# Two groups mixed side by side: q of odd groups on the other half of the partitions, heads collected by halves and crossed once a batch

## The chip, the cores and the metric

The kernel runs on one core of one Trainium2 chip. The metric is device time in microseconds, taken as the median of several runs; lower is better. PE is TensorE, DVE is VectorE, ACT is ScalarE, POOL is GpSimd and SP is SyncE, which here only issues DMAs.

## The reference

Inputs are `u` and `v` (8 batches, 3200 rows, 256 columns), `z` (8, 3200, 64), and the weights `w_q`, `w_k` (256 x 64) and `w_out` (256 x 256), all fp32. For each batch:

```python
attn  = np.maximum(z @ z.T / S, 0) ** 2        # 3200 x 3200
x     = u * (attn @ v)                         # 3200 x 256
q, k  = x @ w_q, x @ w_k                       # 3200 x 64 each
mixed = (q @ k.T / 8) @ x                      # 3200 x 256
out   = np.maximum(mixed, 0) @ w_out
```

There is nothing between q, k and x in the third step that is not linear, so `mixed` is computed as q times the small matrix k.T @ x (64 x 256), which the kernel calls the heads.

## The kernel before

**Stages.** A batch has 3200 rows, cut into 25 blocks of 128 rows and into seven groups: six of 512 rows (0 to 5) and one of 128 (6, `LASTG`). In text, batches are numbered 0 to 7. The main loop runs over phases `k`, some 22 to a batch, in an order that is written out by hand in Python. In a phase, in program order:

- a *mix* of an older batch, if one is due (line 416): its PSUM goes through relu on ACT (`mix_out`, line 428) to a tile `rt`;
- six score matmuls (four in a phase with a mix), in pairs into one PSUM tile (line 211);
- their relu and scale on DVE or ACT into `g` (lines 230, 234), one phase later their square on POOL or ACT into `at` (lines 247, 249);
- the second product, attention times v, from `at` tiles of about two phases earlier or from DMA-transposed ones (`tt`), accumulated in `acc` (line 289). After its first ten matmuls comes an extra: in a phase with a mix the projection of the mixed group with `w_out` (`proj`, line 441; written out by ACT, line 468); in others, where due, `keys_and_heads`;
- when a group of rows is complete, two `gate` operations on DVE multiply by u into `x_sb` (line 315), which frees the `acc` tiles; a DMA transposes `x_sb` into `xT_sb` (line 327).

**Keys, queries and heads.** `keys_and_heads` takes one group, or groups 5 and 6 together. The projection matmuls (line 337) give q on partitions 0 to 63 and k on 64 to 127 of one PSUM tile; ACT copies it to `qk` (line 348), and a DMA transposes that to `kx`, with q in the first 64 columns and k in the last (line 353). At the next key step, `double_keys_queries` has SP copy by DMA the lower half of `qk` over its upper half, so that q stands on both halves (line 361), and POOL copies k over the q columns of `kx` (line 362). The heads matmuls (line 368) then give k.T @ x on both halves. The running sum `ha` is kept by DVE (lines 379, 381); the last addition of a batch gives `hs` in fp16 (line 387), with the same 64 rows on both halves. These DVE operations read the same PSUM tile as ACT's copy to `qk`, and in the trace they start after it.

**Mixes.** A mix takes one group. Two matmuls with 64 contraction rows run on the two halves of the array side by side: columns 0 to 127 of the heads on the lower half, 128 to 255 on the upper. A batch has six, three phases apart or more; the first comes in the phase after the one that makes `hs`. Group 6 is mixed on the side, in the spare columns of a later key step's PSUM tile (`side_mix`, line 481), with all 128 partitions, so that its sum is twice too large and the relu scales by 0.5.

**Slots.** A pool gives each new tile the slot of an older one, and the first writer waits until the older tile's last reader is done. `ps` has three PSUM slots for scores, keys, mixes and projections. `pq` has nine for `qk`, one for each group of seven a batch; `pk` three for `kx`, `prt` three for `rt`.

**The last batch and the tail.** In the last batch a key step comes three phases after its group instead of five, and mixes wait until more than two are listed. After the loop, three mixes of batch 6 are left; they and their projections fill PE while the last groups of batch 7 are gated, transposed and added to its heads by way of x.T @ x (`last_gram`, `last_heads`). Then batch 7 is mixed and projected group by group, with DVE writing out.

Of the kernel before, what the change touches and what calls it, by code (L numbers as in the profile page):

```python
# [9 lines left out]
FP16 = mybir.dt.float16  # L10
FP32 = mybir.dt.float32
RELU = mybir.ActivationFunctionType.Relu
AOP = mybir.AluOpType
# [3 lines left out]
def kernel(  # L17
# [45 lines left out]
    ptt = ctx.enter_context(tc.tile_pool(name="ptt", bufs=1))  # L63
    psml = ctx.enter_context(tc.tile_pool(name="psml", bufs=2))
    pq = ctx.enter_context(tc.tile_pool(name="pq", bufs=9))
    prt = ctx.enter_context(tc.tile_pool(name="prt", bufs=3))
    pps = ctx.enter_context(tc.tile_pool(name="pps", bufs=3, space=bass.MemoryType.PSUM))
    pacc = ctx.enter_context(tc.tile_pool(name="pacc", bufs=1, space=bass.MemoryType.PSUM))

    def ps_tile(name):  # L70
        return pps.tile([P, 2, W], FP32, tag="ps", name=name)
# [77 lines left out]
    wq32 = consts.tile([P, ND, dh], FP32, tag="wq32", name="wq32")  # L149
    wk32 = consts.tile([P, ND, dh], FP32, tag="wk32", name="wk32")  # L150
    wqk = consts.tile([P, ND, 2, dh], FP16, tag="wqk", name="wqk")
    wq2 = consts.tile([P, ND, 2, dh], FP16, tag="wq2", name="wq2")
    wk2 = consts.tile([P, ND, 2, dh], FP32, tag="wk2", name="wk2")
    wo = consts.tile([P, ND, D], FP16, tag="wo", name="wo")
# [8 lines left out]
    def cast_weights():  # L163
        nc.gpsimd.tensor_copy(out=wqk[:, :, 0, :], in_=wq32[:])
        nc.gpsimd.tensor_copy(out=wqk[:, :, 1, :], in_=wk32[:])
        for half in range(2):
            nc.gpsimd.tensor_copy(out=wq2[:, :, half, :], in_=wq32[:])
            nc.gpsimd.tensor_copy(out=wk2[:, :, half, :], in_=wk32[:])
        nc.gpsimd.tensor_copy(out=wo[:], in_=wo32[0][:])
# [174 lines left out]

    def projections_out(b, gi, out):
        gw = widths[gi]
        qks[b, gi] = pq.tile([P, W], FP16, tag="qk", name="qk")
        nc.scalar.copy(out=qks[b, gi][:, 0:gw], in_=out)  # L348

    def turn_keys(b, gi):  # L350
        gw = widths[gi]
        ks[b, gi] = pk.tile([P, 4, 2, dh], FP16, tag="kx", name="kx")
        nc.sync.dma_start_transpose(
            out=ks[b, gi][:, 0 : gw // P, :, :].rearrange("p n a h -> p n (a h)"),
            in_=qks[b, gi][:, 0:gw],
        )

    def double_keys_queries(b, gi):
        gw = widths[gi]
        nn = gw // P  # L360
        nc.sync.dma_start(out=qks[b, gi][dh:P, 0:gw], in_=qks[b, gi][0:dh, 0:gw])
        nc.gpsimd.tensor_copy(out=ks[b, gi][:, 0:nn, 0, :], in_=ks[b, gi][:, 0:nn, 1, :])  # L362

    def heads(b, gis, ps, stop=True):

        parts = [(gi, n) for gi in gis for n in range(widths[gi] // P)]
        for gi, n in parts:
            nc.tensor.matmul(  # L368
                out=ps[:, 1, 0:D],
                lhsT=ks[b, gi][:, n, :, :].rearrange("p a h -> p (a h)"),  # L370
                rhs=xs[b, gi][:, n, :],
                start=((gi, n) == parts[0]),
                stop=(stop and (gi, n) == parts[-1]),
            )

    def heads_out(b, gis, ps):
        if gis[0] == 0:
            hacc[b] = psml.tile([P, D], FP32, tag="ha", name="ha")
            nc.vector.tensor_copy(out=hacc[b][:], in_=ps[:, 1, 0:D])
        elif gis[-1] < LASTG:  # L380
            nc.vector.tensor_add(out=hacc[b][:], in0=hacc[b][:], in1=ps[:, 1, 0:D])  # L381
        else:
            heads_done(b, ps[:, 1, 0:D])

    def heads_done(b, part):
        hss[b] = psml.tile([P, D], FP16, tag="hs", name="hs")
        nc.vector.tensor_add(out=hss[b][:], in0=hacc.pop(b)[:], in1=part)  # L387

    def last_gram(b, gi, ps):
        nj = widths[gi] // P  # L390
# [10 lines left out]
    def last_heads(b, g32, ps):  # L401
        for cc in range(ND):
            nc.tensor.matmul(
                out=ps[:, 1, 0:D],
                lhsT=wk2[:, cc, :, :].rearrange("p t h -> p (t h)"),
                rhs=g32[:, ds(cc * D, D)],
                start=False,
                stop=(cc == ND - 1),
            )

    def mix(b, gi):
        gw = widths[gi]
        ps = ps_tile("mx")
        for db in range(ND):
            half = db * dh
            nc.tensor.matmul(  # L416
                out=ps[:, db, 0:gw],
                lhsT=hss[b][half : half + dh, ds(db * P, P)],
                rhs=qks[b, gi][half : half + dh, 0:gw],
                start=True,  # L420
                stop=True,
            )
        return ps

    def mix_out(b, gi, ps):
        gw = widths[gi]
        rts[b, gi] = prt.tile([P, ND, W], FP16, tag="rt", name="rt")
        nc.scalar.activation(out=rts[b, gi][:, :, 0:gw], in_=ps[:, :, 0:gw], func=RELU)  # L428

    def proj(b, gi, banks=None):  # L430
        rt = rts.pop((b, gi))
# [47 lines left out]
    def side_mix(b, ps):  # L479
        for db in range(ND):  # L480
            nc.tensor.matmul(
                out=ps[:, 1, ds(D + db * P, P)],
                lhsT=hss[b][:, ds(db * P, P)],
                rhs=qks[b, LASTG][:, 0:P],
                start=False,
                stop=(db == ND - 1),
            )

    def side_mix_out(b, ps):
        rts[b, LASTG] = prt.tile([P, ND, P], FP16, tag="rs", name="rs", bufs=2)  # L490
        nc.scalar.activation(
            out=rts[b, LASTG][:].rearrange("p a s -> p (a s)"), in_=ps[:, 1, D : 2 * D],
            func=RELU, scale=0.5,
        )
        side.append((side_proj, side_proj_out, b))

# [13 lines left out]
        nc.sync.dma_start(out=rows(out, b)[:, NT - 1, :], in_=fo[:])  # L510


    todo_mix, todo_between, at_phase, side = [], [], {}, []
    keyed, keyed_at = [], [-9]

    def due(k, fn):
# [11 lines left out]
    def keys_and_heads(b, gis):  # L528

        ps = ps_tile("qk")  # L530
        outs = [ps[:, 0, 0:W], ps[:, 1, D : D + P]]
        projections(b, gis[0], wqk, outs[0])
        aside = None
        if keyed:
            heads(*keyed[0], ps, stop=(len(gis) == 1 and not side))
            if len(gis) > 1:
                projections(b, gis[1], wqk, outs[1], start=False)
            elif side:
                aside = side.pop(0)
                aside[0](aside[2], ps)  # L540
        for gi, o in zip(gis, outs):
            projections_out(b, gi, o)
            turn_keys(b, gi)
        if keyed:
            hb, hgis = keyed.pop(0)
            heads_out(hb, hgis, ps)
            if hgis[-1] == LASTG:
                todo_mix.extend((hb, i) for i in range(LASTG))
                side.append((side_mix, side_mix_out, hb))
        if aside:  # L550
            aside[1](aside[2], ps)
        keyed.append((b, gis))
        keyed_at[0] = now[0]
# [47 lines left out]
    while groups:  # L601
# [3 lines left out]
        n = 4 if k == 0 else 6  # L605
        mixing = None
        if mix_due(k):
            mb, mg = todo_mix.pop(0)
            mixed_at[0] = k
            mixing = (mb, mg, mix(mb, mg))  # L610
            n = 4
        n = min(n, NTILE - produced)
        fresh = []
# [2 lines left out]
        produced += n  # L616
        made_by.append(produced)
        keying = not mixing and key_due(k)
        if keying and keyed:
            for g_ in keyed[0][1]:  # L620
                double_keys_queries(keyed[0][0], g_)
        if mixing:
            mix_out(*mixing)
        staged = []
        act_pair = 0 if (gate_pending or k < 4) else 1
        for i, (p0, sc) in enumerate(fresh):
# [51 lines left out]
        gate_pending = False  # L678
        matmuls = second_product(b, gi, rows_, begins, closes)
        extra = None  # L680
        if mixing:
            mb, mg, _ = mixing

            def extra():
                proj_out(mb, mg, proj(mb, mg), [(False, nc.sync, widths[mg] // P)])
        elif keying:
            extra = todo_between.pop(0)[1]
# [26 lines left out]

    assert not at_phase and not side and not todo_between and len(keyed) == 1
    hb, hgis = keyed.pop()
    for g_ in hgis:
        double_keys_queries(hb, g_)
    psh = ps_tile("hd")
    heads(hb, hgis, psh, stop=False)  # L720
    last_gram(last, LASTG, psg)
    g32 = pg.tile([P, ND * D], FP32, tag="g", name="G")
    nc.scalar.copy(out=g32[:, 0:D], in_=psg[:, 0:D])
    nc.vector.tensor_copy(out=g32[:, D : 2 * D], in_=psg[:, D : 2 * D])
    for mb, mg in todo_mix[:2]:
        mix_out(mb, mg, mix(mb, mg))
    last_heads(last, g32, psh)
    heads_done(last, psh[:, 1, 0:D])
    for mb, mg in todo_mix[2:]:
        mix_out(mb, mg, mix(mb, mg))  # L730

    def store(b, gi, banks=None, ways=None):
        proj_out(b, gi, proj(b, gi, banks), ways or [(True, nc.sync, widths[gi] // P)])

    for i, (mb, mg) in enumerate(todo_mix):
        if i == 0:
            store(mb, mg, [acc_tile(0, "fo0")[:], acc_tile(1, "fo1")[:]],
                  [(True, nc.sync, 2), (True, nc.sync, 2)])
        else:
            store(mb, mg)  # L740
    qs = [(LASTG - 1, ps_tile("qq")[:, 0, :]), (LASTG, acc_tile(0, "qq")[:, 0:P])]
    for gi, o in qs:
        projections(last, gi, wq2, o)
    for gi, o in qs:
        projections_out(last, gi, o)
    mix_out(last, 0, mix(last, 0))
    for gi in range(LASTG - 1):
        mix_out(last, gi + 1, mix(last, gi + 1))
        if gi == LASTG - 2:
            mix_out(last, LASTG, mix(last, LASTG))  # L750
        store(last, gi)
    store(last, LASTG)
    store(last, LASTG - 1, ways=[(False, nc.scalar, 2), (True, nc.sync, 2)])

# [29 lines left out]
```

## Time and profile before

| | |
|---|---|
| median of 3 runs | 807.75 us (806.59 to 809.63) |
| profiled execution | 807.18 us, of which the span is 805.4 us |
| TensorE clock granted, mean | 0.999 of full speed |
| instructions in the span | 16696 |
| DVE, ACT, POOL busy | 493.1, 475.1, 485.2 us |
| DMA q over the upper half (line 361) | 54 issues |
| POOL copy of k (line 362) | 54, 20.4 us busy together |

In a line of the profile's timeline the first number is the start in the span and the second the time to the end of the last instruction of the line, then engine, source line, operation, output<-inputs, shape and count. In brackets stand the idle time of that engine before it and what ended that. Matmuls are pipelined: one of 256 columns shows 0.27 us, but a row of them moves on by about 0.11 us each. PEld is the weight load of TensorE. A line of waits has engine, line and releaser, then us in total, times, and the longest.

### The profile page before, as it was taken

What the parts mean: (1) busy time and instruction counts of PE and PEld (TensorE: products, weight loads), DVE (VectorE), ACT (ScalarE), POOL (GpSimd) and SP (SyncE); (2) the same over time, 40 slices, a digit from 0 to 9 for tenths busy, and PEclk for the clock granted to TensorE, in tenths of its full rate; (3) what the DMA queues carried; (4) which work ended last, traced back from release to release, by engine and by line L of the source; (5) the groups of instructions that cost most, each with busy time, mean ns of one, the idle gap of its engine ahead of it and who ended that gap; (6) DMA issues with size and microseconds to landing.
All of it is one profiled execution on the core that took longest, in us unless ns stands there. A gap on an engine that the chain in (4) does not pass through costs nothing.

```text
span 805.4 us, 16696 instructions
## 1 busy us (share of the span) xinstructions
PE 788.8 (98%) x6778; PEld 584.9 (73%) x6778; DVE 493.1 (61%) x514; ACT 475.1 (59%) x526; POOL 485.2 (60%) x352
## 2 busy tenths in 40 slices
PE   7999999999999999999999999999999999999996
PEld 4777777777777777777777777777777767767774
DVE  5766666565665566755676556765666656655525
ACT  6655556556765556565675556656665565565534
POOL 7957676564666557755666466864676555655420
PEclk9999999999999999999999999999999999999999
DMA  7999899997989969998899979999999996867436
GB/s 175 149 198 192 141 176 181 212 190 134 216 148 208 200 152 194 176 208 186 175 157 211 198 157 178 188 206 175 184 197 157 182 217 143 159 148 183 116 98 246
DMA packets 330878, 143.20 MB, mean 178 GB/s; under 512 B 307441, under 2 KB 313137, under 8 KB 330801
## 3 DMA queue, kind: packets, MB, share of 16 engines
q1 hardware_dynamic: 302528, 125.90, 76.4%
q0 software_dynamic: 28128, 15.98, 17.7%
q8 instruction: 53, 0.87, 0.5%
q10 hardware_dynamic: 144, 0.26, 0.1%
q14 instruction: 25, 0.20, 0.1%
HBM read 59.38 MB, written 26.21 MB: 106 GB/s over the span
## 4 chain that ended last, share of the span: by engine, by line
PE 95%; issue 1%; POOL 1%; DMA 1%; DVE 1%; ACT 0%; SPq 0%; POOLq 0%; DVEq 0%
PE acc L289 69%; PE sc L211 13%; PE fo L441 5%; PE qk L368 3%; PE qk L337 3%; PE mx L416 2%; POOL at L249 1%; DMA z<-in_z_dram 1%; DMA xT_sb<-x_sb 0%; DVE x_sb L315 0%; DVE fo L463 0%; PE qk L499 0%; ACT qk L348 0%; SPq L95 0%; DVE g L234 0%
## 5 line engine op out<-in xcount | busy, mean ns | idle before, releaser
L249 POOL TENSOR_TENSOR at<-g 128x1024 f16<-128x1024 f32 (+2 forms) x234 | 430.3, 1853 | 222.2 <-DVE g L234 136.8
L234 DVE TENSOR_SCALAR g<-sc 128x1024 f32<-128x1024 f32 (+1 forms) x340 | 388.1, 1184 | 188.5 <-PE sc L211 188.1
L289 PE MATMUL acc<-v_sb,at 128*128 128x256 f16 x3656 | 446.8, 273 | 0.4 <-DVE x_sb L315 0.4
L289 PEld LDWEIGHTS <-at 128*128 128x128 f16 x3656 | 344.7, 98 | 108.0 <-issue 66.6
L230 ACT ACTIVATE g<-sc 128x1024 f32<-128x1024 f32 x128 | 131.2, 1025 | 199.6 <-PE sc L211 199.6
L247 ACT ACTIVATE at<-g 128x1024 f16<-128x1024 f32 (+2 forms) x234 | 236.9, 1029 | 0.6 <-DVE g L234 0.6
L289 PE MATMUL acc<-v_sb,tt 128*128 128x256 f16 x1152 | 149.1, 273 | 0.0
L211 PE MATMUL sc<-zT 64*128 64x512 f16 x920 | 129.7, 381 | 2.3 <-DVE hs L387 0.9
L289 PEld LDWEIGHTS <-tt 128*128 128x128 f16 x1152 | 112.5, 98 | 12.9
L315 DVE TENSOR_TENSOR x_sb<-acc,u_sb 128x512 f16<-128x512 f32 (+1 forms) x104 | 69.3, 668 | 66.8 <-PE acc L289 62.5
L428 ACT ACTIVATE rt<-mx 128x1024 f16<-128x1024 f32 (+1 forms) x49 | 49.1, 1012 | 56.8 <-PE mx L416 55.3
L211 PEld LDWEIGHTS <-zT 64*128 64x128 f16 x920 | 34.9, 95 | 50.1 <-issue 28.5
L362 POOL COPY kx<-kx 128x256 f16<-128x256 f16 (+1 forms) x54 | 20.1, 378 | 65.9 <-DMA kx<-qk 65.7
L468 ACT ACTIVATE fo<-fo 128x1024 f32<-128x1024 f32 (+1 forms) x40 | 40.6, 1014 | 24.4 <-PE fo L441 22.6
L441 PE MATMUL fo<-wo,rt 128*128 128x256 f16 x386 | 49.6, 273 | 1.7 <-DVE fo L463 0.9
L348 ACT CAST qk<-qk 128x512 f16<-128x512 f32 (+1 forms) x54 | 28.7, 545 | 27.5 <-PE qk L368 13.2
L441 PEld LDWEIGHTS <-rt 128*128 128x128 f16 x386 | 37.2, 98 | 7.5 <-ACT rt L428 1.9
L381 DVE TENSOR_TENSOR ha<-ha,qk 128x256 f32<-128x256 f32 x31 | 13.1, 421 | 30.0 <-ACT qk L348 30.0
L368 PE MATMUL qk<-x_sb,kx 128*128 128x256 f16 x191 | 28.4, 273 | 1.9 <-POOL kx L362 1.9
L337 PE MATMUL qk<-xT_sb,wqk 128*128 128x512 f16 (+1 forms) x108 | 29.9, 358 | 0.0
L368 PEld LDWEIGHTS <-kx 128*128 128x128 f16 x195 | 19.0, 98 | 14.2 <-POOL kx L362 2.4
L289 PE MATMUL acc<-v_sb,ttl 128*128 128x256 f16 x192 | 22.6, 273 | 0.0
(47 smaller groups left out, 150.2 us busy)
## 6 DMA issues: line engine op xcount, KB each, us to landing
u_sb<-in_u_dram SPq DMA_DIRECT2D x48, 512.0 KB, 4.8
out_dram<-fo SPq DMA_DIRECT2D x46, 512.0 KB, 4.2
v_sb<-in_v_dram POOLq DMA_DIRECT2D x35, 320.0 KB, 5.7
qk<-qk SPq DMA_DIRECT2D x47, 64.0 KB, 4.0
zd<-in_z_dram POOLq DMA_DIRECT2D x7, 400.0 KB, 8.1
tt<-at SPq DMA_TRANSPOSE x146, 4.3
u_sb<-in_u_dram SPq DMA_DIRECT2D x8, 128.0 KB, 3.0
xT_sb<-x_sb SPq DMA_TRANSPOSE x56, 4.1
```

Of the source, the lines that this page charges most:

```text
L211: nc.tensor.matmul(out=sc[:, h, 0:gw], lhsT=zT[b][half : half + dqk, ts(ti, P)], rhs=zT[b][half : half + dqk, ds(gs, gw)], start=True, sto ...
L230: nc.scalar.activation(out=g[:, hs, 0:w], in_=sc[:, hs, 0:w], func=RELU, scale=GSCALE)
L234: nc.vector.tensor_scalar(out=g[:, hs, 0:w], in0=sc[:, hs, 0:w], scalar1=0.0, scalar2=GSCALE, op0=AOP.max, op1=AOP.mult,)
L247: nc.scalar.square(out=out, in_=g[:, hs, 0:w])
L249: nc.gpsimd.tensor_mul(out=out, in0=g[:, hs, 0:w], in1=g[:, hs, 0:w])
L289: nc.tensor.matmul(out=accs[j // 2][:, ds((j % 2) * D, D)], lhsT=weights(b, gi, ti, j), rhs=vs[b][:, ti, :], start=(first and ti == rows_[ ...
L315: nc.vector.tensor_mul(out=xs[b, gi][:, 2 * half : 2 * half + n, :].rearrange("p n d -> p (n d)"), in0=accs[half][:, 0 : n * D], in1=us[b, ...
L337: nc.tensor.matmul(out=out, lhsT=w[:, ac, :, :].rearrange("p t h -> p (t h)"), rhs=xTs[b, gi][:, 0 : gw // P, ac, :], start=(start and ac ...
L368: nc.tensor.matmul(out=ps[:, 1, 0:D], lhsT=ks[b, gi][:, n, :, :].rearrange("p a h -> p (a h)"), rhs=xs[b, gi][:, n, :], start=((gi, n) == ...
L428: nc.scalar.activation(out=rts[b, gi][:, :, 0:gw], in_=ps[:, :, 0:gw], func=RELU)
L441: nc.tensor.matmul(out=banks[jf // 2][:, ds((j - jf) * D, D)], lhsT=rt[:, dc, ts(j, P)], rhs=wo[:, dc, :], start=(dc == 0 and j == jf), st ...
L468: nc.scalar.mul(out=flat_out[:, sl], in_=part, mul=FINAL_SCALE)
```

## The change

- For groups 1, 3, 5 and 6 (`swapped`) the projection weights are `wkq` instead of `wqk`: k stands on the lower half, q on the upper. Nothing is doubled any more: the DMA of line 361 and the POOL copy of line 362 go.
- The heads matmuls give the heads on one half only (the half that holds k), q.T @ x on the other, which is not used. DVE keeps the sum of even groups on the upper half of `ha` and that of odd groups and 6 on the lower. Once a batch `heads_done` copies each half across into `hx`, adds `ha` and `hx` to `hs`, and copies the upper half of `hs` to `hz`, a tile whose lower half is zero.
- A mix takes a pair of groups, even and odd side by side, and 128 columns of the heads; six mixes a batch as before, two for each pair. A group is projected only when both mixes of its pair are done, from a list `todo_proj`, one in each mix phase that has one.
- `side_mix` reads `hz` and no longer scales by 0.5.
- `qk` of group 6 has two slots of its own, of 128 columns; the other groups share the nine of `pq`. `rt` is a tile for a pair, with two slots.
- Four POOL operations join the weight casts (two casts to `wkq`, two memsets of `hz`).
- In the tail, the crossing of the last batch's sum is done ahead of `last_heads`, one of the first two mixes' relus of batch 7 is on DVE, and the projections follow the pairs.

```diff
-    prt = ctx.enter_context(tc.tile_pool(name="prt", bufs=3))
+    prt = ctx.enter_context(tc.tile_pool(name="prt", bufs=2))
...
+        nc.gpsimd.tensor_copy(out=wkq[:, :, 1, :], in_=wq32[:])
+        nc.gpsimd.tensor_copy(out=wkq[:, :, 0, :], in_=wk32[:])
+        for tile_ in hz:
+            nc.gpsimd.memset(tile_[0:dh, :], 0.0)
...
     def projections_out(b, gi, out):
-        qks[b, gi] = pq.tile([P, W], FP16, tag="qk", name="qk")
+        if gi < LASTG:
+            qks[b, gi] = pq.tile([P, W], FP16, tag="qk", name="qk")
+        else:
+            qks[b, gi] = pq.tile([P, P], FP16, tag="ql", name="ql", bufs=2)
...
-    def double_keys_queries(b, gi):
-        gw = widths[gi]
-        nn = gw // P
-        nc.sync.dma_start(out=qks[b, gi][dh:P, 0:gw], in_=qks[b, gi][0:dh, 0:gw])
-        nc.gpsimd.tensor_copy(out=ks[b, gi][:, 0:nn, 0, :], in_=ks[b, gi][:, 0:nn, 1, :])
+    def swapped(gi):
+        return gi % 2 == 1 or gi == LASTG
...
     def heads_out(b, gis, ps):
+        mine = slice(0, dh) if swapped(gis[0]) else slice(dh, P)
...
-        elif gis[-1] < LASTG:
-            nc.vector.tensor_add(out=hacc[b][:], in0=hacc[b][:], in1=ps[:, 1, 0:D])
+        acc, part = hacc[b][mine, :], ps[mine, 1, 0:D]
+        if gis[0] < 2:
+            nc.vector.tensor_copy(out=acc, in_=part)
         else:
-            heads_done(b, ps[:, 1, 0:D])
+            nc.vector.tensor_add(out=acc, in0=acc, in1=part)
+    def heads_crossed(b):
+        hx = psml.tile([P, D], FP32, tag="hx", name="hx", bufs=1)
+        nc.vector.tensor_copy(out=hx[0:dh, :], in_=hacc[b][dh:P, :])
+        nc.vector.tensor_copy(out=hx[dh:P, :], in_=hacc[b][0:dh, :])
+        return hx
+    def heads_done(b):
+        hx = heads_crossed(b)
         hss[b] = psml.tile([P, D], FP16, tag="hs", name="hs")
-        nc.vector.tensor_add(out=hss[b][:], in0=hacc.pop(b)[:], in1=part)
+        nc.vector.tensor_add(out=hss[b][:], in0=hacc.pop(b)[:], in1=hx[:])
+        nc.vector.tensor_copy(out=hz[b % 2][dh:P, :], in_=hss[b][dh:P, :])
...
-    def mix(b, gi):
+    def mix(b, pair, db):
+        ps = ps_tile("mx")
+        for a in range(2):
+            half = a * dh
+            nc.tensor.matmul(
+                out=ps[:, a, :],
+                lhsT=hss[b][half : half + dh, ds(db * P, P)],
+                rhs=qks[b, 2 * pair + a][half : half + dh, :],
+                start=True, stop=True,
+            )
+        return ps
...
             if hgis[-1] == LASTG:
-                todo_mix.extend((hb, i) for i in range(LASTG))
+                heads_done(hb)
+                todo_mix.extend((hb, i, db) for i in range(LASTG // 2) for db in range(ND))
...
-        if keying and keyed:
-            for g_ in keyed[0][1]:
-                double_keys_queries(keyed[0][0], g_)
         if mixing:
             mix_out(*mixing)
+            if mixing[2] == 1:
+                todo_proj.extend((mixing[0], 2 * mixing[1] + a) for a in range(2))
...
-        if mixing:
-            mb, mg, _ = mixing
+        if mixing and todo_proj:
+            mb, mg = todo_proj.pop(0)
...
+    heads_out(hb, hgis, psx)
+    hx = heads_crossed(last)
+    nc.vector.tensor_add(out=hx[:], in0=hx[:], in1=hacc.pop(last)[:])
...
+    while todo_mix:
+        mix_next()
+    store(*todo_proj.pop(0), [acc_tile(0, "fo0")[:], acc_tile(1, "fo1")[:]],
+          [(True, nc.sync, 2), (True, nc.sync, 2)])
+    while todo_proj:
+        store(*todo_proj.pop(0))
...
+    for pair in range(LASTG // 2):
+        for db in range(ND):
+            mix_out(last, pair, db, mix(last, pair, db), on_dve=(pair == 0 and db == 1))
+            if pair:
+                store(last, 2 * pair - 2 + db)
+    last_mix(last)
```

## The prediction

> **What bounds the kernel now.** First the page of the profile: busy time by engine and the chain that ended last.
>
> ```profile
> PE 788.8 (98%) x6778; PEld 584.9 (73%) x6778; DVE 493.1 (61%) x514; ACT 475.1 (59%) x526; POOL 485.2 (60%) x352
> PE 95%; issue 1%; POOL 1%; DMA 1%; DVE 1%; ACT 0%; SPq 0%; POOLq 0%; DVEq 0%
> ```
>
> TensorE sets the time from start to end; the other engines have four tenths of the span free. So an edit on DVE, GpSimd, ACT or a DMA queue counts only where TensorE stands still for it. Where does it stand still now? The list of waits has few places (engine, line, releaser: us in total, times, longest):
>
> ```profile
> PEld L289 <- POOL at L249: 2.8, 7, 0.4
> PE qk L368 <- POOL kx L362: 1.9, 1, 1.9
> PE sc L211 <- DVE hs L387: 0.9, 1, 0.9
> ```
>
> Of what the change takes away (54 DMAs of q, 54 GpSimd copies of k, 20.4 us busy), only the second line is a stall of TensorE. The instructions of TensorE itself stay the same in number and shape: six mixes of two matmuls a batch, as before. So the gain is small from the outset, and the question is which new waits come. I then read, in order of time, the stretch from `heads` to the first mix in each batch, the start around the weight casts, the last batch and the tail.
>
> **1. The head sum grows a chain of DVE operations, and it meets GpSimd.** Before, one DVE addition (L387) ends the heads and the next phase opens with a mix that reads `hs`. After, that addition is followed by two copies across the halves and a second addition before `hs` exists; then a copy to `hz`. In the batch that begins at 330 us:
>
> ```profile
> 329.49 1.90 POOL L249 TENSOR_TENSOR at<-g 128x1024 f16<-128x1024 f32 x1
> 329.64 0.42 DVE L387 TENSOR_TENSOR hs<-ha,qk 128x256 f16<-128x256 f32 x1 [0.58 <-ACT qk L348]
> 329.98 1.85 DVE L134 COPY zd<-zd 128x1600 f16<-128x1600 f16 x1
> 331.32 0.39 PE L416 MATMUL mx<-qk,hs 64*128 64x512 f16 x2
> ...
> 232.69 0.58 DVE L134 COPY zd<-zd 128x1600 f16<-128x1600 f16 x1
> ```
>
> The same copy, SBUF to SBUF, takes 0.58 us when GpSimd is idle (its operation ended at 232.75) and 1.85 us when a GpSimd multiply is running: it ends at 331.83, 0.44 us after that multiply (331.39). So such a copy waits for the whole running GpSimd operation. The Trainium skill states this as a lock (SBUF — State Buffer, Who interferes with whom): a DVE operation in a two-port mode and a GpSimd operation exclude each other for a whole instruction; the row agrees. It adds that a DVE operation with two SBUF inputs is excluded too while GpSimd reads; no row here shows one, and it would give the same sum, since GpSimd is idle by the time of the second addition.
>
> The cross copies stand exactly where the 1.85 us copy stands now. Their own length: the one DVE copy of 256 fp32 elements from SBUF took 294 ns (L109); an addition of 256 takes 421 ns; PE started 0.06 us after the `hs` that it waited for at 718.0. Of the waiting copy, 0.58 - 0.44 = 0.14 us was spent ahead of the wait, so copy one ends 0.15 us after GpSimd, copy two 0.29 later, the addition 0.42, PE 0.06: 0.92 us after the multiply's end. First mixes, and the end of the GpSimd operation that runs then: 138.50 (136.76), 234.03 (232.75), 331.32 (331.39), 428.60 (428.72), 525.89 (525.95), 627.52 (627.76). (The seventh, of batch 6, comes 15 us after its head sum.) The first two have 0.8 and 0.35 us to spare: nothing. The next four wait 0.99, 1.04, 0.98 and 1.16: **+4.2 us**. These GpSimd operations follow their `g` tiles (ACT's, ended 327.50, for the multiply at 327.63), not the copies of k that go, so they stay where they are. Behind the waiting copies DVE holds the z copy and the first stages of the next phase; these slip with PE by the same microsecond and cost nothing more. Bounds: without that wait, `hs` is there at 330.06 + 0.29 + 0.29 + 0.42 + 0.06 = 331.12, before the mix: 0. If a second GpSimd multiply slipped in between, 1.9 us more in each of the four: 11.8. I take 4.2, by the row of the z copy, which is the nearest.
>
> **2. The slots of q.** A new `qk` tile needs one of nine slots. This bites once now, at the first keys of the last batch:
>
> ```profile
> 716.53 0.39 PE L416 MATMUL mx<-qk,hs 64*128 64x512 f16 x2
> 716.97 0.59 ACT L348 CAST qk<-qk 128x512 f16<-128x512 f32 x1 [2.65 <-PE mx L416]
> 717.58 0.42 DVE L387 TENSOR_TENSOR hs<-ha,qk 128x256 f16<-128x256 f32 x1 [3.08 <-ACT qk L348]
> 718.06 0.39 PE L211 MATMUL sc<-zT 64*128 64x512 f16 x2 [0.92 <-DVE hs L387]
> 718.66 0.38 PE L289 MATMUL acc<-v_sb,at 128*128 128x256 f16 x2 [0.21 <-DVE x_sb L315]
> 719.26 1.03 PE L289 MATMUL acc<-v_sb,at 128*128 128x256 f16 x8 [0.22 <-DVE x_sb L315]
> ```
>
> ACT's copy waits for the next mix to free a slot; behind it stand the head sum and two gates on DVE, and the PSUM tile that the scores need. From mix to the third product 719.26 - 716.53 = 2.73 us pass, against 0.97 in an undisturbed phase (764.32 mix, 765.07 products, two of them 0.22): a loss of 1.76 us. Counting live tiles by the times of keys and mixes gives nine there and at most eight elsewhere, so the count explains the trace. In the new order a tile of a pair lives until the second mix of its pair, while the short group's tile has slots of its own. Counted again: at 713.5 eight are live, no wait. At 729.7 nine (two of batch 5, six of batch 6, one of batch 7), and the next release is the mix at 733.62. At 760.5 nine, released by the mix at 764.32. Elsewhere at most eight. In both places the shape is that of the fence: ACT's copy from the mix's end (+0.43), 0.59, head sum 0.42, then two gates of 0.6 to 0.7, third product 2.7 us after the mix. **+3.5 us** for two; bounds 2.2 (the scores' wait alone, 1.1 each) and 5 (ACT's side copy of 0.38, mix copies and transposes queued behind ACT's copy on ACT and SP also late). The old loss goes, but DVE has the two copies, an addition and the `hz` copy before the gates, some 1.2 us, so the gates end near 718.3 rather than 719.2: **-0.9 us** (0 to -1.76).
>
> **3. The keys' stall.**
>
> ```profile
> 655.92 0.39 POOL L362 COPY kx<-kx 128x256 f16<-128x256 f16 x1 [8.60 <-DMA kx<-qk]
> 656.37 0.61 PE L368 MATMUL qk<-x_sb,kx 128*128 128x256 f16 x4 [1.90 <-POOL kx L362]
> ```
>
> PE could have gone on at 654.30. The copy and its hand-over (0.45 us) go; the transpose was issued at 649.00, behind the q DMA that took SP from 648.42, and may land 0.58 us sooner: **-1.0 us** (-0.45 if DMA traffic and not SP's order made it late, -2.1 if all goes). SP is otherwise relieved of 54 issues of 0.54 us that nobody waits for.
>
> **4. The start.** Four GpSimd operations join the weight casts: two casts at 0.24 us each from start to start (30.06, 30.30, 30.54), two memsets of 64x256, between the 206 ns of 128x128 and 0.31 if length counts fully, 0.26 taken: 1.0 us.
>
> ```profile
> 30.06 0.29 POOL L164 CAST wqk<-wq 128x128 f16<-128x128 f32 x1
> 39.84 1.91 POOL L249 TENSOR_TENSOR at<-g 128x1024 f16<-128x1024 f32 x1
> 41.86 2.52 PEld L289 LDWEIGHTS <-at 128*128 128x128 f16 x24 [0.42 <-POOL at L249]
> ```
>
> GpSimd has no gap from 30.06 to 41.75, and the weight load at 41.86 is released by the multiply that ends there. **+0.9 us** (0 if PE's normal phase gap of 0.42 hides it, 1.0 at most). By 42.70 GpSimd has 0.96 us of slack again.
>
> **5. The tail and the late projection.** A pair can be projected only after its second half, so the first mix phase (138.5) has no projection (-0.87 us, the eight matmuls at 140.35), and the tail has four leftover groups instead of three. I stepped the tail through with the rows of before (mix 0.33, projection 0.87 to 0.98, DVE 1.22 for 1024 columns, ACT 1.02): the fourth group adds 0.9 us of PE; the DVE-side relu of the last batch, queued behind four evacuations, lets the first projection go near 793 rather than 791.2, of which the two engines' parallel relu wins back a part; the last evacuation ends 0.7 us later. Together **-0.2 us** (-1.0 to +1.5).
>
> Other edits at nothing: head sums on 64 partitions have the same 256 columns; the side mix with `hz` has the same shape; `hz` is read a key step later, hidden behind some 15 us.
>
> **The sum.** 4.2 + 3.5 - 0.9 - 1.0 + 0.9 - 0.2 = +6.5 us. The profiled execution took 807.18 us (span 805.4), so 813.7; the median of the three runs stands 0.57 above it, so **814.2 us**.
>
> **Rivals.** (a) *The cross copies don't wait for GpSimd*, and `hs` comes 0.2 us ahead of the mix. For it: the z copy is fp16, and no fp32 copy is seen to wait. Against: 294 ns for 256 elements is well under the 421 of an addition of as many, so it seems to run in a faster way, as the z copy does (1600 elements in 580). It decides at 331.32: `hs` at 331.12 or 332.3. Time 814.2 - 4.2 = 810.0, not slower as far as can be told. (b) *The slots don't bite*, the release coming another way than I count: 810.7. Against: the count finds the one wait that the trace has. (c) *The relief wins*: neither wait comes and terms 2 to 5 fall at their best ends: 0 - 1.76 - 2.1 + 0 - 1.0 = -4.9, 802.9. Against: TensorE has little idle time to give back. (d) *A second GpSimd operation gets in* between the copies, as GpSimd no longer waits for keys (65.7 us in 18 waits): +7.6, 821.8. Against: after 331.39 GpSimd waits until 333.34 for DVE's `g`.
>
> **How the numbers follow.** A measurement of this kernel tells 0.5% (4.0 us) from no change, so slower means above 811.8. Forecast 0.64 (0.05 of it below that line, if several small terms fall low); (a) 0.12 and (b) 0.08, nearly all within the line; (c) 0.05, faster; (d) 0.11, slower. Slower 0.72, same 0.23, faster 0.05. The range takes in (a), (b) and the forecast's own spread, and leaves out (c) and most of (d): 809 to 819.5.
>
> **What would show it.** Right: in four batches a mix released by DVE's `hs`, about 1 us each, with cross copies that end just after a GpSimd multiply; ACT's copy of q released by a mix near 734 and near 765, none near 717; the heads near 656 waiting under 1.5 us, for a DMA; the weight load near 42 a microsecond later. Wrong: cross copies of 0.3 us beside a running multiply; no `hs` among PE's releasers; or a second wait inside the cross chain.

## The result, and the profile after

The changed kernel takes **812.93 us** (median of 11 runs, 812.36 to 813.33) against 808.94 us (11 runs, 805.08 to 812.61) for the kernel before on the same chip: a ratio of **1.0056, interval 1.0039 to 1.0073**. It is slower, and the time lies within the forecast (814.2 us, 809 to 819.5). The difference is smaller than forecast: 4.0 us between these medians, 0.56%, where 6.5 us, 0.8%, were forecast, which is above the interval. Part of that lies in where the forecast started: the median of the kernel before was 807.75 in three runs and is 808.94 in eleven. The terms of the forecast were read off one profiled execution and are compared here with another: the one of after took 812.93 us, its span 811.2, which is 5.8 us over the 805.4 of before.

The page of the profile after, busy time and the chain that ended last by engine:

```profile
PE 789.1 (97%) x6778; PEld 585.0 (72%) x6778; DVE 507.0 (63%) x548; ACT 473.3 (58%) x524; POOL 468.6 (58%) x302
PE 94%; DVE 3%; ACT 1%; issue 0%; DMA 0%; DVEq 0%; ACTq 0%
```

TensorE does the same work (6778 matmuls, 0.3 us more busy time). GpSimd lost 16.6 us of work and ACT 1.8, which by itself saves no time; DVE gained 13.9 us and now holds 3% of the last chain, where it held 1%. The difference is standstill of TensorE, and the list of waits has it (engine, line, releaser: us in total, times, longest):

```profile
PEld L435 <- DVE hs L405: 4.3, 5, 1.4
PE mx L435 <- DVE hs L405: 3.1, 3, 1.1
PE sc L217 <- ACT rs L533: 1.3, 1, 1.3
PE sc L217 <- DVE ha L393: 0.9, 1, 0.9
```

The two first are the head sum, seen once by the weight load and once by the matmul (the same idle time, not to be added); the two last are the phases in which ACT waits for a slot of q. The line `PE qk L368 <- POOL kx L362` of before has no successor. To place the 5.8 us I compared when TensorE reaches the same mix or key step in both traces; the difference, after minus before, is called the drift below.

| place | forecast | measured |
|---|---|---|
| cross chain, mixes near 331, 428, 526, 628 | +4.2 | +3.3 (1.04, 0.0, 1.04, 1.21) |
| slots of q, near 734 and 765 | +3.5 | +3.8 (1.93, 1.86) |
| old slot wait at 717 | -0.9 | -0.83 |
| keys at 656 | -1.0 | -2.08 |
| start, weight casts | +0.9 | -0.46 (no loss, below) |
| first projection gone | -0.87 | -0.87 |
| tail, to the end of the span | +0.7 | +2.92 |
| sum | +6.5 | +5.8 |

The drift is -0.46 at 47 us, -1.33 after the first mix phase, +1.96 at 629, -0.12 at 658, -0.96 at 729, +2.83 at 772, +3.98 at DVE's last evacuation (its last copy of a PSUM tile to SBUF, from which it is stored) and +5.8 at the end of the span.

**The cross chain.** The timeline of after, the batch whose first mix stands near 331:

```profile
328.15 1.89 POOL L255 TENSOR_TENSOR at<-g 128x1024 f16<-128x1024 f32 x1
328.75 1.45 DVE L398 COPY hx<-ha 64x256 f32<-64x256 f32 x1
330.22 0.29 DVE L399 COPY hx<-ha 64x256 f32<-64x256 f32 x1
330.55 0.42 DVE L405 TENSOR_TENSOR hs<-ha,hx 128x256 f16<-128x256 f32 x1
331.03 0.39 PE L435 MATMUL mx<-qk,hs 64*128 64x512 f16 x2 [0.98 <-DVE hs L405]
```

GpSimd's multiply ends at 330.04. The first copy ends at 330.20 though it began at 328.75; the second, with nothing on GpSimd beside it, takes 0.29. The mix starts 0.99 us after the multiply's end; the prediction had 0.92 (0.15, 0.29, 0.42, 0.06: it lacked the 0.03 between two DVE operations). In the batch near 428 the same chain meets no multiply:

```profile
424.65 1.89 POOL L255 TENSOR_TENSOR at<-g 128x1024 f16<-128x1024 f32 x1
427.08 0.29 DVE L398 COPY hx<-ha 64x256 f32<-64x256 f32 x1
428.31 0.39 PE L435 MATMUL mx<-qk,hs 64*128 64x512 f16 x2
```

**The slots.** The phase at 734, PE and ACT:

```profile
732.66 0.39 PE L435 MATMUL mx<-qk,hs 64*128 64x512 f16 x2
733.09 0.59 ACT L357 CAST qk<-qk 128x512 f16<-128x512 f32 x1 [3.52 <-PE mx L435]
734.60 0.39 PE L217 MATMUL sc<-zT 64*128 64x512 f16 x2 [1.33 <-ACT rs L533]
735.51 1.03 PE L295 MATMUL acc<-v_sb,at 128*128 128x256 f16 x8 [0.19 <-DVE x_sb L321]
```

ACT's copy starts 0.43 us after the mix that frees its slot, as it did near 717 in the trace of before; the third product comes 2.85 us after the mix (forecast 2.7). The same stands near 765, with `ha` in place of `rs` as the scores' releaser.

**The tail.** DVE's last evacuation and the store that it releases, after (SPq is SyncE issuing a DMA, with the time that the issue holds its queue):

```profile
804.48 0.69 DVE L505 TENSOR_SCALAR fo<-fo 128x512 f32<-128x512 f32 x1 [0.21 <-ACT fo L510]
805.20 0.80 SPq L511 DMA_DIRECT2D out_dram<-fo  x1
```

The evacuation ends at 805.17; before, it ended at 801.19. Of the 3.98 us between them 2.83 are drift brought along and 1.15 arise in the tail. From there to the end of the span it is 6.0 us, where before it was 4.2.

### The profile page after: what moved, and what is told of

Same layout as the page of the kernel before. It is cut to its first block, busy times and chain, and to the rows that moved or that the text cites. A ratio compares the mean times of both kernels' runs of the same rounds, so it can differ in the third digit from the quotient of the medians.

```text
span 811.2 us, 16564 instructions
## 1 busy us (share of the span) xinstructions
PE 789.1 (97%) x6778; PEld 585.0 (72%) x6778; DVE 507.0 (63%) x548; ACT 473.3 (58%) x524; POOL 468.6 (58%) x302
## 4 chain that ended last, share of the span: by engine, by line
PE 94%; DVE 3%; ACT 1%; issue 0%; DMA 0%; DVEq 0%; ACTq 0%
PE acc L295 68%; PE sc L217 14%; PE fo L483 5%; PE qk L343 3%; PE qk L377 3%; PE mx L435 2%; DVE fo L505 1%; DVE hx L398 1%; DVE x_sb L321 0%; ACT qk L357 0%; PE ztp L118 0%; DMA z<-in_z_dram 0%; ACT g L236 0%; DVE hs L405 0%; DVE ha L393 0%
## 5 line engine op out<-in xcount | busy, mean ns | idle before, releaser
L456 ACT ACTIVATE rt<-mx 128x1024 f16<-128x1024 f32 x47 | 48.0, 1024 | 60.1 <-PE mx L435 58.5
L357 ACT CAST qk<-qk 128x512 f16<-128x512 f32 x47 | 27.5, 586 | 29.4 <-PE qk L377 13.3
L393 DVE TENSOR_TENSOR ha<-ha,qk 64x256 f32<-64x256 f32 x30 | 12.6, 419 | 28.1 <-ACT qk L357 22.5
L435 PE MATMUL mx<-qk,hs 64*128 64x512 f16 x96 | 18.5, 386 | 3.7 <-DVE hs L405 3.1
L127 POOL DMA_DIRECT2D v_sb<-in_v_dram x35 | 20.9, 596 | 0.0
```

What stands on the lines that cost most here:

```text
L435: nc.tensor.matmul(out=ps[:, a, :], lhsT=hss[b][half : half + dh, ds(db * P, P)], rhs=qks[b, 2 * pair + a][half : half + dh, :], start=Tru ...
L456: nc.scalar.activation(out=out, in_=ps[:], func=RELU)
```

## The experiments

The theory: two new waits make the loss, DVE's cross copies held back by a running GpSimd multiply, and ACT's copy of q held back by a slot of `pq`; the tail makes the rest, and the keys' stall gives some back. The rivals are named with each run. Ratios are to the kernel before, with their intervals.

**One slot more in the changed kernel.**

```diff
-    pq = ctx.enter_context(tc.tile_pool(name="pq", bufs=9))
+    pq = ctx.enter_context(tc.tile_pool(name="pq", bufs=10))
```

> The changed kernel with ten slots for q instead of nine, nothing else. Slot theory: the two waits of ACT's copy of q for a later mix (near 734 and 766 in the changed kernel) are gone, with the 1.93 and 1.86 us that TensorE fell behind there, so the span falls from 811.2 to about 807.4 (3.8 us less). Rival (the loss comes from the head sum's longer way through DVE or from the gates behind it, not from the slots): the losses near 734 and 766 stay, span near 811.

Measured: 809.06 us, 1.0022 (1.0007 to 1.0038); span 807.0. ACT's waits for a mix are gone from the list, and so are the scores' waits for `rs` and `ha`; the drift stays at -0.81 through 775 us. The three waits for `hs` are as they were. So the slots cost about 3.9 us in the median (812.93 to 809.06, from separate sets of runs); up to 775 us the drift of the two traces differs by 3.6, or 3.8 once their first key step is set equal.

**The cross copies on ACT.**

```diff
-        nc.vector.tensor_copy(out=hx[0:dh, :], in_=hacc[b][dh:P, :])
-        nc.vector.tensor_copy(out=hx[dh:P, :], in_=hacc[b][0:dh, :])
+        nc.scalar.copy(out=hx[0:dh, :], in_=hacc[b][dh:P, :])
+        nc.scalar.copy(out=hx[dh:P, :], in_=hacc[b][0:dh, :])
```

> The changed kernel with the two cross copies on ACT instead of DVE. Port theory (a DVE copy from SBUF to SBUF waits for the running GpSimd multiply): no copy waits any more, a copy on ACT takes some 0.4 us whether GpSimd runs or not, so hs is ready 0.42 + 2 x 0.35 + 0.42 = about 1.6 us after the head addition starts, against 1.7 us until the mix: the waits of 1.0 to 1.2 us of the mixes near 331, 526 and 629 go, span about 808 (3.2 us less). If the second addition, with two SBUF inputs, also waits for the multiply (the Trainium skill says so), hs is ready some 0.4 us after the multiply's end and each of the three mixes still waits 0.4 to 0.7: span about 809.5. Rival (the chain is just too long, GpSimd has no part in it): the three waits stay near 1.0 or grow, span 811 or more.

Measured: 811.18 us, 1.005 (1.003 to 1.0069); span 809.8. The waits for `hs` shrink to 0.33, 0.33 and 0.49 us but stay, for another reason. The timeline of this kernel, same batch:

```profile
328.58 1.89 POOL L255 TENSOR_TENSOR at<-g 128x1024 f16<-128x1024 f32 x1
329.18 0.40 ACT L399 COPY hx<-ha 64x256 f32<-64x256 f32 x1
329.61 1.14 DVE L405 TENSOR_TENSOR hs<-ha,hx 128x256 f16<-128x256 f32 x1 [0.47 <-ACT hx L399]
```

ACT's copies are not held back: they take 0.40 us in every batch, with a multiply beside them or not. The addition is: 1.14 us instead of 0.42, ending at 330.75, 0.28 us after the multiply ends at 330.47. The addition, too, then, waits for a running multiply; this was the case that the prediction left as one that no row showed. The Trainium skill (SBUF — State Buffer, Who interferes with whom) states that a DVE instruction with two SBUF inputs contends with a GpSimd instruction that reads SBUF, and that ACT waits on nobody; this trace agrees on both, with 1.14 against 0.42 and with the 0.40 of ACT's copy.

**No multiply beside the chain.** In the phase with a batch's first mix, the third square goes to ACT instead of GpSimd; DVE's chain is as long as ever.

```diff
-            second_on_act = [False, True, k % 2 == 0]
+            second_on_act = [False, True, k % 2 == 0 or (mixing is not None and mixing[1:3] == (0, 0))]
```

> The changed kernel with one GpSimd multiply fewer in the phase of each batch's first mix (its third pair squared by ACT), so that GpSimd is idle when the cross copies run; the copies stay on DVE. Port theory: the cross copy takes 0.29 us in every batch, hs is ready 0.3 us ahead of the mix, the three waits of 1.0 to 1.2 us go, span about 808. Rival (chain too long by itself): the three mixes still wait about 1 us, span near 811. Should ACT's extra square of 1.05 us make a weight load wait, that is seen as a new releaser ACT and the gain is smaller.

Measured: 809.5 us, 1.0041 (1.0026 to 1.0057); span 807.0. No mix waits for `hs` any more:

```profile
328.53 0.29 DVE L398 COPY hx<-ha 64x256 f32<-64x256 f32 x1
328.85 0.29 DVE L399 COPY hx<-ha 64x256 f32<-64x256 f32 x1
329.17 0.42 DVE L405 TENSOR_TENSOR hs<-ha,hx 128x256 f16<-128x256 f32 x1
```

The whole crossing takes 1.06 us and is done by 329.59. The drift stays at -1.54 through 642 us. The median is 3.4 us better, as much as the three waits made (3.3). The length of the chain alone, the rival, is ruled out.

**Mixes and a projection moved from the tail into the loop.** The second mix of batch 6's middle pair and one more projection go into the loop's last phase with a mix.

```diff
+            if mixing[:3] == (last - 1, 1, 0):
+                todo_mix.pop(0)
+                mix_out(last - 1, 1, 1, mix(last - 1, 1, 1))
+                todo_proj.extend((last - 1, g) for g in (2, 3))
...
+                if (mb, mg) == (last - 1, 1):
+                    mb2, mg2 = todo_proj.pop(0)
+                    proj_out(mb2, mg2, proj(mb2, mg2), [(False, nc.sync, 4)])
```

> The changed kernel with the second half of batch 6's middle pair mixed, and one more group projected, in the last mix phase of the loop, so that the tail has three leftover groups again as in the kernel before instead of four. Theory (the fourth group's evacuation and the output stores that it pushes together at the end cost more than its matmuls): the loop ends 1.2 us later, the tail gets 2.5 to 3 us shorter, the last store lands 4.2 instead of 6.0 us after DVE's last evacuation starts to be issued; span 809.5 to 810. Rival (work is only moved; the late last landing in the changed kernel's profile is chance): span 811, the last landing as likely late as not.

Measured: 812.23 us, 1.0068 (1.0047 to 1.0089); span 810.2. Counted from the first key step of each trace, the loop ends 1.1 us later and the last evacuation 0.4 earlier (804.95). The gain over the kernel after is 0.7 us: the rival, work that only moves, is nearer.

**A shorter way to the last heads.** The last product of the heads takes a PSUM tile of the accumulators, and ACT evacuates one leftover projection of DVE's.

```diff
-    psh = ps_tile("hd")
+    psh = acc_tile(1, "hd")[:].rearrange("p (a d) -> p a d", a=2)
...
-        store(*todo_proj.pop(0))
+        store(*todo_proj.pop(0), None, [(len(todo_proj) != 1, nc.sync, 4)])
```

> The changed kernel with two edits in the tail: last_heads writes into the second acc tile, which is free, instead of a new PSUM slot that must wait for a relu; and the second of the three leftover evacuations on DVE is on ACT, which is idle then. Theory (the tail lost because last_heads waits 0.98 us for a slot, and because DVE's relu of batch 7 stands behind four evacuations): first projection of batch 7 about 1 us earlier, span about 810.2. Rival (the tail is held by the order of relus and evacuations after that, or by the output stores): less than 0.4 us.

Measured: 812.47 us, 1.0068 (1.0041 to 1.0094); span 811.0. The heads wait 0.44 us instead of 0.98. DVE's first evacuation of batch 7 starts at 797.55 instead of 797.42, but this trace runs 0.5 us late from its first key step on; with that taken off, it comes 0.4 us sooner. The median gains 0.5 us. So most of the shorter wait reaches the end, but it is less than half of what the theory had, and near the rival's 0.4: TensorE's wait was a small part of what the tail lost.

**One slot more in the kernel before.** Same edit as the first, in the kernel before.

> The kernel before with ten slots for q instead of nine. Slot theory: the one wait of ACT's copy of q near 717 goes, with the 1.76 us that the prediction counted for it; nothing else changes; span about 803.7 instead of 805.4. Rival (the loss there comes from the gates, which would be as late without it): span 805.

Measured: **804.68 us, 0.9967 (0.9943 to 0.999)**: faster than both kernels. The wait near 717 is gone (drift +0.71 ahead of it, -1.04 behind it, so 1.75 us; the prediction had 1.76). So the slot is a fault of the kernel before that the change made twice as dear.

**Why were the keys late?** Three kernels, all from the kernel before. In the first the q DMA is issued from ACT's queue instead of SP's; in the second it is left out (the upper half of `qk` then still holds k, and half of the mixed columns are not what they should be); in the third the GpSimd copy of k is left out (with the same loss of half of the columns).

```diff
-        nc.sync.dma_start(out=qks[b, gi][dh:P, 0:gw], in_=qks[b, gi][0:dh, 0:gw])
+        nc.scalar.dma_start(out=qks[b, gi][dh:P, 0:gw], in_=qks[b, gi][0:dh, 0:gw])
```

> The kernel before with the DMA that copies q over the upper half issued from ACT's queue instead of SP's. Theory (SP's queue is in order, and these 54 DMAs, each waiting for the transposed keys, made SP run some 4 us late near 640 us and so the keys' transpose near 650): the stall of 2.1 us near 656 goes or shrinks below 0.5, though the GpSimd copies of k are still there, and the runs of the kernel scatter less; 54 issues of some 0.4 us on ACT cost nothing as ACT has four tenths free, unless ACT itself then waits for the keys' transpose and holds up relus: that would show as TensorE waiting for ACT. Span 803 to 804. Rival (the stall is the GpSimd copy of k, late in GpSimd's queue, and no matter of SP): the stall stays near 2, span 805.

> The kernel before without the DMA that copies q over the upper half (left out altogether: the mixes then read k there, so half of the mixed columns are not what they should be; all else is in place, the GpSimd copy of k too). If these DMAs make the keys' transposes land late, be it by SP's order or by their traffic, the waits of the heads for keys go (2.1 us near 656, and others of 1 to 2 us that come and go), median some 2 us lower, 805, and less scatter. If the copy of k on GpSimd is what counts, the heads still wait 1.5 to 2 us near 656 and the median stays near 807.

> The kernel before without the GpSimd copy of k (left out altogether: the heads' lower half then holds q against x, so half of the mixed columns are not what they should be; the DMA of q stays). The copy comes 0.3 us after the keys land and takes 0.4, so if the landing is late by itself, the heads near 656 wait 0.45 us less, 1.0 to 1.6 us instead of 1.5 to 2.1, now for the DMA; median 806.5 against 807. If GpSimd held in its queue by the wait (65.7 us in 18 waits) is what makes things late, through the squares and their transposes that SP then issues late, the wait goes altogether, median 805.

Measured, in this order: 807.85 us, 1.0015 (0.9993 to 1.0037); **804.93 us, 0.9969 (0.9951 to 0.9987)**; 809.01 us, 1.0013 (0.9992 to 1.0034). With the DMA on ACT's queue the stall near 656 stays (first fence). That kernel also pays for the move: ACT, in whose queue the DMA waits for the transposed keys, stands idle for 5.3 us up to 656.25, and TensorE then loses 1.15 us behind ACT's late operations (drift -0.28 to +0.87). Without GpSimd's copy the heads still wait, now for the transpose itself, 1.40 us near 370 and 2.24 us near 567 (second fence); near 656, where TensorE is by then 4.0 us later than in the kernel before, they don't. Of the three, only the kernel without the DMA has no heads matmul that waits.

```profile
655.64 0.39 POOL L362 COPY kx<-kx 128x256 f16<-128x256 f16 x1 [8.39 <-DMA kx<-qk]
656.09 0.39 PE L368 MATMUL qk<-x_sb,kx 128*128 128x256 f16 x2 [1.69 <-POOL kx L362]
```

```profile
567.12 0.50 PE L367 MATMUL qk<-x_sb,kx 128*128 128x256 f16 x3 [2.24 <-DMA kx<-qk]
```

The queue of SP tells more. Here is the transpose that the heads near 656 need, in the kernel before and then after:

```profile
648.42 0.48 SPq L361 DMA_DIRECT2D qk<-qk  x1
649.00 1.36 SPq L353 DMA_TRANSPOSE kx<-qk  x1
```

```profile
646.88 1.20 SPq L362 DMA_TRANSPOSE kx<-qk  x1
```

| kernel | issued at | landed after |
|---|---|---|
| before | 649.00 | 6.9 |
| before, q DMA from ACT's queue | 648.76 | 6.8 |
| before, without the q DMA | 647.35 | 6.4 |
| after | 646.88 | 4.0 |

From 612 to 650 us SP in the kernel before goes from one issue to the next without a pause over 0.12 us, three q DMAs among them (0.47, 0.59, 0.48). Without them the transpose is issued 1.65 us sooner; in the kernel after SP even has a pause, 634.45 to 635.97. With them on ACT's queue SP is 1.88 us ahead when it comes to the z transpose (638.73 against 640.61), but that issue takes 6.64 us there, 4.47 in the kernel before and 5.99 without the DMAs, and the transpose of the keys leaves only 0.24 us sooner. So in these executions it counts that the DMAs are there, not which queue issues them. What stretches SP's issues, and why the transpose also lands sooner after its issue in the kernel after, these traces do not tell; it stays open.

**All mends together.** The tenth slot, the square on ACT and the shorter tail, in the kernel after.

> The changed kernel with ten slots for q, ACT squaring the third pair in the phase of a batch's first mix, and the tail of the next run. If the losses are separate they add: 811.2 - 3.8 - 3.3 - 1.0 = span about 803.1, median about 804.7, faster than the kernel before by some 0.3%. Rival (the losses hide one another, or ACT's extra squares cost as TensorE runs ahead): span 805 or more.

Measured: 805.41 us, 0.9993 (0.9971 to 1.0016). The gains over the kernel after (3.9, 3.4 and 0.5) would give 805.1, so they nearly add. The profiled execution of this one, 807.27 us, still had one wait for keys, 1.76 us near 467, although no q DMA is left in it.

**And batch 7 begun earlier.** As the last, but the first pair of batch 7 is mixed between the leftover projections of batch 6, with its relus on ACT, and DVE evacuates all of the leftovers again.

```diff
+    store(*todo_proj.pop(0))
+    for db in range(ND):
+        mix_out(last, 0, db, mix(last, 0, db))
...
-    for pair in range(LASTG // 2):
+    for pair in range(1, LASTG // 2):
```

> The changed kernel with ten slots for q, ACT squaring the third pair in the phase of a batch's first mix, last_heads in the free acc tile, and batch 7's first pair mixed between the leftover projections, both relus on ACT, which is idle then, so that its projections need not wait for relus queued behind the last q copies and behind DVE's evacuations. Theory (the tail is late because the first projection of batch 7 needs two relus): DVE's first evacuation of batch 7 comes 1.5 to 2 us earlier than in the run with ten slots and the other tail (there 4.6 us after the last key matmuls start, 792.2 in that run), its end and the last store about 1.5 us earlier: median 804.0, clearly faster than the kernel before. Rival (DVE's evacuations and the output stores set the end, whatever comes first): gain under 0.5 us, median 805.

Measured: **804.98 us, 0.9963 (0.9947 to 0.9978)**, span 803.3: faster than the kernel before and the kernel after. Against the version ahead of it that is 0.4 us: the first evacuation of batch 7 comes 0.47 us sooner, once that kernel's stall is taken off, and the span ends 5.6 us after the last evacuation. Moving TensorE's work about gains little there, as its rival said.

## Why the prediction was right, and where its steps were not

**Cross chain: right in mechanism, one of its four batches wrong.** Three of the four cost 1.04 to 1.21 us against 0.98 to 1.16; the fourth (428) cost nothing. The step that failed is "these GpSimd operations follow their `g` tiles, not the copies of k that go, so they stay where they are". That was read off at 327.50, one batch, and taken over to the others. At 428 GpSimd stood for keys until 422.92 in the kernel before and then ran three multiplies in a row, at 423.13, 424.98 and 426.83. With the copy of k gone they run at 420.94, 422.80 and 424.65; the last ends at 426.54, ahead of the copies at 427.08. So a part of the relief did help here. Rivals (a) and (d) fall: fp32 copies do wait, and no second multiply got in. Of (c) two terms came at or near its ends (keys, start), but both waits came too.

**Slots: right.** The count of live tiles found both places and the shape of the stall; 3.8 us against 3.5, and -0.83 against -0.9 for the old one. Rival (b) falls.

**The keys' stall: too small.** It gave 2.1 us, the best end of the bounds, not 1.0. The step that failed is that the transpose "may land 0.58 us sooner" and that SP's other 54 issues are such "that nobody waits for": SP had no pause for some 37 us, so three issues had piled up ahead of this transpose: without them it left 1.65 us sooner, and 2.1 us sooner in the kernel after.

**The start: wrong, 0.9 us.** The four operations delay GpSimd by 1.0 us, as sized, and the memset of 64x256 takes 0.30 (0.25 from start to start). But TensorE loses nothing:

```profile
40.37 1.91 POOL L255 TENSOR_TENSOR at<-g 128x1024 f16<-128x1024 f32 x1
41.40 2.52 PEld L295 LDWEIGHTS <-at 128*128 128x128 f16 x24 [0.42 <-issue]
```

The multiply ends at 42.28, and the weight loads begin at 41.40 and run through without a pause, 2.52 us as before: they did not need that tile. The releaser that the row of before named was the end nearest to a gap of 0.42 that is there anyway. The prediction's lower bound, 0 "if PE's normal phase gap of 0.42 hides it", was the right value. The -0.46 of drift at 47 us arises in the first 13 us, among the first loads; it is no gain, as the other seven kernels made from the one after have -0.68 to +0.05 there.

**The tail: the largest miss, 2.92 us where the term was 0.7.** The missing projection gave its 0.87. The last evacuation comes 1.15 us later, where the step says that it "ends 0.7 us later", and a step is lacking altogether, the store: the prediction counted to DVE's last evacuation and took what follows as unchanged. It grew by 1.8 us, from 4.2 to 6.0: the last store lands 5.03 us after its issue, where it was 3.15. The traces show what most of this comes with. Below, the first line is DMA's count of one queue from 799.7 to 801.7 in the kernel after, the second the same from 788.5 to 790.5 in the kernel before (packets, MB, share of the sixteen DMA engines); the third is a stretch at the end of the kernel after, whose last two numbers are DMA's busy share and GB/s:

```profile
q8 instruction: 1, 0.02, 6.0%
q8 instruction: 1, 0.02, 5.4%
808.40:809.90 1.50, 0.00 (x0) 0.00 (x0) 0.00 (x0) 0.00 (x0) 0.00 (x0) 0.50 0.07 25
```

One packet of 16 KB that carries instructions starts at 799.76 in the kernel after and holds a DMA engine for 1.92 us (6.0% of sixteen engines in 2 us), in the midst of the last stores. Even the first of these, issued at 798.68 with nothing else under way, takes 5.08 us, and all that follow 4.7 to 5.1. At the end about one engine of the sixteen works alone for 1.5 us, at 25 GB/s against 388 just before. In the kernel before the packet comes at 788.60: the two stores behind it take 4.3 and 4.1 us, the last eight 2.6 to 3.2, and no engine works alone for more than 0.1 us. The seven other kernels made from the one after have the packet among the last stores too, 0.9 to 1.4 us of one engine alone, and 5.3 to 5.7 us from the last evacuation to the end. Of the four made from the kernel before, three have it ahead of the last eight stores, with 0.1 us alone and 4.1 to 4.2 us to the end, and the one without GpSimd's copy has it among them at 798.26, with 0.3 and 4.5. So the packet goes with some 1.4 of the 1.8 us; the rest fits the stores' closer issue (the last eight within 6.5 us, before within 7.7). No run moved the packet by itself, so that it is the cause is read from the traces, not tested.

The errors have both signs: -0.9 (one batch), -1.1 (keys) and -1.4 (start) against +0.3 (slots), +0.1 (old wait) and +2.2 (tail), which is -0.8 together, as 5.8 stands to 6.5. So the total, 1.3 us off in the median, is better than its terms, and that is in part luck: without the 1.8 us of the last store, which no term foresaw, the span would have grown by 4.0. The kernel before itself scatters, 804.6 to 813.7 over 30 runs on one chip, where the kernel after stays within 1 us; since the kernel without the q DMA stays within 0.9 us in eleven of its twelve, the key steps that are late in some executions are the likely reason. The DMAs can't be all of it: the kernel with the square on ACT and the one with all mends, which have none, are 2 to 7 us above the median in three of twelve executions each.

## What to carry to other kernels

Where TensorE is busy 98% of the span, relief of other engines is worth only the stalls it ends, and any new dependence ahead of a matmul can cost more: price it by what GpSimd runs at that moment, since here DVE's SBUF-to-SBUF copies and two-input additions waited for a running multiply (1.45 us instead of 0.29, 1.14 instead of 0.42), and ACT's copies did not (0.40). When a change lengthens the life of a tile, count the live tiles against the slots at every allocation; here one slot was worth 3.9 us after and, without the change at all, made the kernel before faster. A small DMA on a queue that never pauses is late work for all that stands behind it (1.65 us here for three), and moving it to another queue need not help: there it may hold that engine's own work. A forecast that ends with the last operation lacks the last store.

## What was not expected of the hardware

- A DVE addition of 128x256 with both inputs in SBUF took 1.14 to 1.30 us beside a GpSimd multiply, 0.42 without.
- 54 small DMAs from SBUF to SBUF (47 of 64 KB, 7 of 16 KB; in the median 4.0 and 3.0 us from issue to landing) cost 2.6 us in the median (807.49 to 804.93), though no wait of TensorE names one of them; issued from another queue they gave a time that can't be told from the kernel before's, with a new wait of ACT in it.
- The span ends 4.1 to 4.5 us after DVE's last evacuation in one form of the tail and 5.3 to 6.0 in the other. With the longer times one 16 KB packet of instructions, which holds a DMA engine for 0.9 to 1.9 us, stands among the last stores.
